# Routed experts in a fused attention and mixture-of-experts kernel: a hold on SP's queue before the second expert's second matrix, one packed load of the counts, and the third block's transposes moved behind the second block

## Chip, core and metric

The kernel runs on one core of one Trainium2 chip. The metric is the time of one execution on the device in microseconds; less is better.

## What is computed

Three stages follow one another: windowed attention over 1152 tokens, a dense mixture of four experts, and a routed mixture of eight experts. The change touches the third stage alone, which in the reference is (cut):

```python
    skip_score = x @ w_skip
    do_compute = skip_score > 0
    out = x.copy()
    ...
    xc = x[do_compute]
    logits = xc @ w_gate
    e_idx = np.argmax(logits, axis=1)
    ...
    for e in range(E):                       # E = 8
        mask = e_idx == e
        ...
        h = np.maximum(xc[mask] @ w1[e], 0.0)    # 512 -> 1024
        y[mask] = gate_w[mask, None] * (h @ w2[e])   # 1024 -> 512
    out[do_compute] = xc + y
```

How many tokens an expert gets is known only on the chip. All matrices are float32.

## The kernel before

**Tiling.** Each float32 operand is split in a high and a low part (`xs` for tokens, `wa1h`/`wa1l`, `wa2h`/`wa2l`, `wb1h`... for weights), and a product is made of three passes of TensorE. Experts use two sets of weight tiles in turn: even experts `wb`, odd ones `wa`. A matrix comes from memory in four loads of 512 KB (lines L314 and L316, tile `raw`, issued by SP); ScalarE casts each load to the high part (L330) and VectorE subtracts to get the low part (L334).

**Blocks.** The routed tokens of an expert are taken in blocks of 128 rows. A block is: gather its rows from the scratch tensor `scr` by an indirect DMA of GpSimd (L869; tile `xg` for an expert's first and second block, `xj` for its third), transpose them on TensorE (L362, four instructions), split them into `xs` (L896 on ScalarE, L898 on VectorE), first product (L920), ReLU into `hr` (L944, ScalarE), transpose `hr` (L961), split into `ht` (L965, L968), second product (L920 again), scale and add (L1004), and scatter to the output (L877, GpSimd). In a block, 24 matmuls of the first product in two halves of 12 come with two groups of transposes of `hr` and 24 matmuls of the second product. An expert's second and third block stand in `tc.If`: `over(e, i)` tests if the expert has more than 64 times i rows. A block with at most 64 rows takes a smaller variant. In this execution experts 1, 2 and 4 have a second block (small for expert 2), and expert 4 alone a third one (small).

**Order.** A planner (`Plan`) collects operations with priorities and estimated durations and writes each engine's instructions in the order of its estimated starts when `plan.run()` is called; each engine then runs its own queue strictly in order and waits for semaphores. One call covers an expert's first block together with the loads and splits of the next expert's weights; each conditional block is planned by itself. The rows of the third block were transposed in the conditional second block by `amid`, which puts them into the plan between that block's two products, with priority 11.5 and a dependence on `("g2", 2)`. As names of the plan are forgotten at each `plan.run()` and the second product is added later, that dependence names nothing there, and the priority (the groups of the first product have 11, 12, ...) decides the place.

**Counts.** VectorE writes three packed numbers to `cnt`: the levels of all experts, whether any expert has over 384 rows, and the same or a second block of the last expert. `counts` (L1072) loads each into a register on all five engines. The branches read them. `ahead` gives TensorE's sequencer a hint on the coming branch.

**Around the change.** When routing is done, at about 488 us, the first block of expert 0 starts at once with rows that were picked on TensorE. In parallel GpSimd issues seven gathers, the first of them for expert 1's first block. SP issues the four loads of expert 1's second matrix (`raw2` buffers, L316), and after the branch of expert 0 the four loads of expert 2's first matrix (L314).

## Time and profile before

| | us |
|---|---|
| median of 3 runs | 666.32 (663.26 to 671.25) |
| the profiled execution: its time | 669.26 |
| the profiled execution: its span | 667.5 |
| PE busy | 632.6 (95%) |
| DVE busy | 314.6 (47%) |
| ACT busy | 234.5 (35%) |
| POOL busy | 75.5 (11%) |

The profile comes from one execution. PE is TensorE's matmuls, PEld its weight loads, DVE VectorE, ACT ScalarE, POOL GpSimd, and SP the engine that only issues DMAs; a "q" behind a name is the engine's sequencer. A wait's releaser is inferred from semaphores; "remote" is a release whose origin the profile doesn't tell. The granted clock is TensorE's, as a share of 2.4 GHz; 0.5 is 1.2 GHz. Idle time counts only where the engine is the one that the end waits for.

### The profile page before, as it was taken

To read this page: it belongs to the slowest core of one execution; us is meant where nothing else is said; L and a number is where in the kernel's file an instruction comes from. 1 tells how busy PE (TensorE), PEld (TensorE's weight loads), DVE (VectorE), ACT (ScalarE), POOL (GpSimd) and SP (SyncE) were. 2 spreads that over 40 slices of the span, in tenths; PEclk is the share of its full clock that TensorE was granted. 3 is DMA by queue.
4 is the path that set the end of the run, shared out by engine and by line. 5 is a ranking of instruction groups with operands and counts; after the bars stand their busy time and mean duration, and the time that the engine had idled before them with its cause. 6 is when DMAs were issued, how large, how long until landed. Compare 5 with 4: busy or idle time off the path is not lost. (4 is left out here: it accounts for less than half of the span.)

```text
span 667.5 us, 9890 instructions
## 1 busy us (share of the span) xinstructions
PE 632.6 (95%) x3787; PEld 553.6 (83%) x3787; DVE 314.6 (47%) x683; ACT 234.5 (35%) x488; POOL 75.5 (11%) x104
## 2 busy tenths in 40 slices
PE   8889999999999999999999999999997899969974
PEld 6688898898989898989898989889876677858864
DVE  5878731127412125412125426165856564931961
ACT  5668630026302024202023311114326464823741
POOL 3112320000000000000000000000123122230510
PEclk9989999999999999999999999999997899979987
DMA  9892100006400004300003310010559864970730
GB/s 217 208 286 66 33 3 1 0 1 229 149 1 1 0 1 130 122 1 0 1 1 126 127 64 33 31 64 13 190 177 373 302 188 159 325 281 18 236 108 11
DMA packets 55770, 71.44 MB, mean 107 GB/s; under 512 B 32932, under 2 KB 32932, under 8 KB 55696
## 3 DMA queue, kind: packets, MB, share of 16 engines
q1 hardware_dynamic: 52912, 62.17, 29.5%
q0 software_dynamic: 2784, 8.30, 4.3%
q8 instruction: 43, 0.70, 0.4%
q14 instruction: 31, 0.25, 0.1%
HBM read 63.74 MB, written 7.47 MB: 107 GB/s over the span
## 5 line engine op out<-in xcount | busy, mean ns | idle before, releaser
L523 PE MATMUL mm<-xth,wa1h 128*128 128x384 f32 (+1 forms) x416 | 137.6, 331 | 0.0
L523 PE MATMUL mm<-xtl,wa1h 128*128 128x384 f32 (+1 forms) x416 | 135.8, 327 | 0.0
L523 PE MATMUL mm<-xth,wa1l 128*128 128x384 f32 (+1 forms) x416 | 135.7, 326 | 0.0
L529 ACT ACTIVATE hh<-mm 128x384 fp32r<-128x384 f32 (+1 forms) x104 | 48.4, 466 | 236.2 <-PE mm L523 231.2
L544 PE MATMUL mm<-wa2h,hh 128*128 128x512 f32 (+1 forms) x296 | 117.3, 396 | 0.0
L531 DVE SCALAR_TENSOR_TENSOR hl<-mm,hh 128x384 fp32r<-128x384 f32 (+1 forms) x104 | 54.6, 526 | 128.4 <-ACT hh L529 128.1
L544 PE MATMUL mm<-wa2h,hl 128*128 128x512 f32 (+1 forms) x296 | 115.1, 389 | 0.0
L544 PE MATMUL mm<-wa2l,hh 128*128 128x512 f32 (+1 forms) x296 | 115.0, 388 | 0.0
L523 PEld LDWEIGHTS mm<-xth,wa1h 128*128 128x128 f32 x416 | 79.0, 190 | 0.6 <-issue 0.2
L523 PEld LDWEIGHTS mm<-xtl,wa1h 128*128 128x128 f32 x416 | 78.9, 190 | 0.4
L523 PEld LDWEIGHTS mm<-xth,wa1l 128*128 128x128 f32 x416 | 78.9, 190 | 0.0
L544 PEld LDWEIGHTS mm<-wa2h,hl 128*128 128x128 f32 x296 | 55.7, 188 | 12.4
L544 PEld LDWEIGHTS mm<-wa2h,hh 128*128 128x128 f32 x296 | 55.8, 188 | 11.2
L544 PEld LDWEIGHTS mm<-wa2l,hh 128*128 128x128 f32 x296 | 55.8, 189 | 11.0
L556 DVE SCALAR_TENSOR_TENSOR x<-mm,prob,x 128x512 f32<-128x512 f32 x24 | 18.0, 751 | 86.8 <-PE mm L544 86.8
L781 POOL DMA_INDIRECT x<-scr,id x1 | 2.0, 1970 | 385.0 <-DVE id L798 385.0
L334 DVE TENSOR_TENSOR wa2l<-raw,wa2h 128x1024 fp32r<-128x1024 f32 x32 | 38.6, 1218 | 7.8 <-ACT wa2h L330 7.8
L330 ACT CAST wa2h<-raw 128x1024 fp32r<-128x1024 f32 x32 | 33.0, 1051 | 25.9 <-PE mm L544 18.6
L334 DVE TENSOR_TENSOR wa1l<-raw,wa1h 128x1024 fp32r<-128x1024 f32 x32 | 38.6, 1236 | 2.1 <-ACT wa1h L330 2.1
L330 ACT CAST wa1h<-raw 128x1024 fp32r<-128x1024 f32 x32 | 32.0, 1048 | 17.4 <-DMA raw<-in_moe_w_dram 9.1
L968 DVE SCALAR_TENSOR_TENSOR ht<-pt,ht 128x512 fp32r<-128x512 f32 (+2 forms) x27 | 15.1, 568 | 36.4 <-ACT ht L965 32.7
L920 PE MATMUL mm<-wa1h,xs 128*128 128x512 f32 (+1 forms) x60 | 22.4, 437 | 6.9 <-issue 3.5
(209 smaller groups left out, 887.4 us busy)
## 6 DMA issues: line engine op xcount, KB each, us to landing
raw<-in_moe_w_dram SPq DMA_DIRECT2D x96, 512.0 KB, 5.9
qn<-in_q_dram SPq DMA_DIRECT2D x8, 256.0 KB
kn<-in_k_dram SPq DMA_DIRECT2D x8, 256.0 KB, 5.9
vn<-in_v_dram SPq DMA_DIRECT2D x8, 256.0 KB
scr<-x SPq DMA_DIRECT2D x8, 256.0 KB
out_dram<-x SPq DMA_DIRECT2D x8, 256.0 KB, 2.3
qn<-in_q_dram SPq DMA_DIRECT2D x2, 128.0 KB, 3.3
kn<-in_k_dram SPq DMA_DIRECT2D x2, 128.0 KB
```

What stands on the lines that cost most here:

```text
L330: (POOL.tensor_copy if hpool else DVE.tensor_copy if hdve else ACT.copy)(out=aps()[0], in_=b.tile)
L334: (POOL if pool else DVE).tensor_tensor(out=l, in0=b.tile, in1=f32(h), op=ALU.subtract)
L523: PE.matmul(out=ps[:, 0:n], lhsT=wa[a][:, kk, f * 128:(f + 1) * 128], rhs=x[:, kk, g0:g0 + n], start=(i == 0), stop=(i == 3 * KC - 1))
L529: add("ACT", c_act(n), lambda: ACT.activation(out=hh[:, f, 0:n], in_=ps[:, 0:n], func=ACTF.Relu), rd=[ps], wr=[("hh", f)], prio=-1)
L531: add("DVE", c_dve(n), lambda: DVE.scalar_tensor_tensor(out=hl[:, f, 0:n], in0=ps[:, 0:n], scalar=0.0, in1=f32(hh[:, f, 0:n]), op0=ALU.max ...
L544: PE.matmul(out=ps[:, 0:c1 - c0], lhsT=x[:, f, o:o + 128], rhs=wa[a][:, f, c0:c1], start=(f == 0 and i == 0), stop=(f == FC - 1 and i == 2))
L556: DVE.scalar_tensor_tensor(out=z, in0=y, scalar=prob[:, t, e:e + 1], in1=z, op0=ALU.mult, op1=ALU.add)
L781: add("POOL", 1.0, lambda: POOL.indirect_dma_start(out=R["x0"], out_offset=None, in_=scr[0:128 * (GT + 1), :], in_offset=bass.IndirectOffs ...
L920: PE.matmul(out=ps[:, 0:cols.stop - cols.start], lhsT=op(k), rhs=ring[f"{c}{a}"][:, k, cols], start=(n == 0 and k == ks[0] and a == "h"), ...
L968: add("DVE", c_dve(w * n), lambda: DVE.scalar_tensor_tensor(out=ht[:, s, n:2 * n], in0=p[:, 0:w, 0:n], scalar=0.0, in1=f32(ht[:, s, 0:n]), ...
```

## The change

Four edits in the routed stage. A one-element DMA (`hold`) from the gathered rows of expert 1's first block into a scratch tensor `pins` is put on SP's queue ahead of expert 1's second matrix, and the gather of those rows is named earlier in the code (it stays the first on GpSimd's queue). The three register loads become one, and the two flags are worked out from the packed levels by register arithmetic (`many`, `further`); `num` on VectorE loses two instructions, and the load's planned place is earlier (`slack` 1.5 for 4.0). The third block's transposes are added behind the second block, in the full variant as before, and depend on the fourth group of the second product, `("g2", 3)`. The gathers' loop skips the one that was named earlier.

```diff
+    pins = scr_p.tile([128, 16], F32, name="pins")
...
-            DVE.tensor_reduce(out=sm[:, 1:2], in_=x[:, 5], axis=AX.X, op=ALU.max)
-            DVE.tensor_tensor(out=sm[:, 2:3], in0=sm[:, 1:2], in1=x[:, 1, E2 - 1:E2], op=ALU.max)
...
-            DVE.tensor_copy(R["cnt"][0:1, E2:E2 + 3], sm)
+            DVE.tensor_copy(R["cnt"][0:1, E2:E2 + 1], sm)
...
         w_pass("r", 1, 1)
+        xgs[1, 0] = gather(1, 0)
+
+        def hold():
+
+            SP.dma_start(out=pins[0:1, 0:1], in_=xgs[1, 0].tile[0:1, 0:1])
+
+        add("SP", 0.5, hold, rd=[xgs[1, 0]], wr=["MR"], slack=-2.5)
         w_pass("r", 1, 2)
...
         def counts():
-            for i, m in ((E2, 8 ** E2 - 1), (E2 + 1, 1), (E2 + 2, 1)):
-                nv.append(nc.values_load(R["cnt"][0:1, i:i + 1], min_val=0, max_val=m,
-                                         skip_runtime_bounds_check_because="levels of all experts, packed"))
+            nv.append(nc.values_load(R["cnt"][0:1, E2:E2 + 1], min_val=0, max_val=8 ** E2 - 1,
+                                     skip_runtime_bounds_check_because="levels of all experts, packed"))
+
+        def many():
+
+            return (nv[0] >> 1) & (nv[0] >> 2) & sum(8 ** e for e in range(E2))
...
-            def gathered():
-                if e == E2 - 1:
-                    xgs[e, 2] = gather(e, 2)
-                third["xt"] = xpose(xgs[e, 2], 11.5, [("g2", 2)])
-
             with tc.If(over(e, 2 * j + 1)) as c:
-                block(e, j, x, xt, amid=gathered if j == 1 else None)
+                if j == 1 and e == E2 - 1:
+                    xgs[e, 2] = gather(e, 2)
+                block(e, j, x, xt)
+                if j == 1:
+                    third["xt"] = xpose(xgs[e, 2], 11.5, [("g2", 3)])
...
-            return nv[2] > 0 if e == E2 - 1 else over(e, 2)
+            return (many() | (nv[0] & (6 * 8 ** e))) > 0 if e == E2 - 1 else over(e, 2)
...
-                    with tc.If(nv[1] > 0):
+                    with tc.If(many() > 0):
                         deep()
...
-                add("X", 0.0, counts, rd=["cnt"], wr=["nv"], slack=4.0)
+                add("X", 0.0, counts, rd=["cnt"], wr=["nv"], slack=1.5)
...
-                    if e + d < E2:
+                    if e + d < E2 and (e + d, j) not in xgs:
```

TensorE's queue in the second block of expert 1 (`xs` its rows, `xj` the third block's), before, from the third matmul of the first product to the transposes of `hr`:

```order
L920 MATMUL mmx<-wa1h,xs 128x512
L920 MATMUL mmx<-wa1l,xs 128x512
L362 MATMUL pt<-ident,xj 128x128 [waits DMASW5_49,PE_49]
L362 MATMUL pt<-ident,xj 128x128 x3
L920 MATMUL mmx<-wa1h,xs 128x512
L920 MATMUL mmx<-wa1l,xs 128x512
L920 MATMUL mmx<-wa1h,xs 128x512
L920 MATMUL mmx<-wa1l,xs 128x512
L920 MATMUL mmx<-wa1h,xs 128x512 x5
L920 MATMUL mmx<-wa1l,xs 128x512
L920 MATMUL mmx<-wa1h,xs 128x512
L920 MATMUL mmx<-wa1l,xs 128x512
L961 MATMUL pt<-ident,hr 128x128 [waits DVE_49,Activation_49]
```

And in the changed kernel, at the end of the same block's second product, up to the branch on a third block:

```order
L920 MATMUL mmx<-wa2h,ht 128x512 [waits Activation_49]
L920 MATMUL mmx<-wa2l,ht 128x512
L920 MATMUL mmx<-wa2h,ht 128x512
L920 MATMUL mmx<-wa2l,ht 128x512
L364 MATMUL pt<-ident,xj 128x128 [waits DMASW5_49,PE_49]
L364 MATMUL pt<-ident,xj 128x128 x3
L920 MATMUL mmx<-wa2h,ht 128x512
L920 MATMUL mmx<-wa2l,ht 128x512
L920 MATMUL mmx<-wa2h,ht 128x512
L920 MATMUL mmx<-wa2l,ht 128x512
L920 MATMUL mmx<-wa2h,ht 128x512 [waits DVE_49]
L920 MATMUL mmx<-wa2h,ht 128x512 x3
```

The transposes with their wait for the gather (`DMASW5`) stood behind the fourth matmul of the block; they now stand behind the fortieth of 48, with eight matmuls to follow.

SP's queue behind the last rows of the dense stage, before (`raw` with a number are the four loads of expert 1's second matrix):

```order
L316 DMA raw_4271<-in_moe_w_dram 128x2x512 [waits DMAHW1_49,DMAHW0_49,DMAHW3_49,DMASW0_49,DMAHW4_49,PE_49,DMAHW7_49,Activation_49,Pool_49]
L316 DMA raw_4291<-in_moe_w_dram 128x2x512
L1072 TENSOR_LOAD cnt [waits DMAHW2_49,DMAHW3_49,DMAHW1_49,DMAHW4_49,DMAHW0_49,DMAHW5_49,DVE_49,DMAHW6_49,PE_49,DMAHW7_49,Activation_49,Pool_49]
L1072 TENSOR_LOAD cnt x2
L316 DMA raw_4331<-in_moe_w_dram 128x2x512
L316 DMA raw_4363<-in_moe_w_dram 128x2x512 [waits DMAHW2_49]
```

And in the changed kernel, at the same place:

```order
L1078 TENSOR_LOAD cnt [waits DMAHW2_49,DMAHW3_49,DMAHW1_49,DMAHW4_49,DMAHW0_49,DMAHW5_49,DVE_49,DMAHW6_49,PE_49,DMAHW7_49,Activation_49,Pool_49]
L1070 DMA pins<-xg 1x1 [waits DMAHW3_49,DMAHW1_49,DMAHW4_49,DMAHW0_49,DMAHW7_49,DMASW1_49,PE_49]
L318 DMA raw_4363<-in_moe_w_dram 128x2x512 [waits PE_49,DMASW0_49,Activation_49,Pool_49]
L318 DMA raw_4378<-in_moe_w_dram 128x2x512
L318 DMA raw_4382<-in_moe_w_dram 128x2x512 [waits DMAHW2_49]
L318 DMA raw_4387<-in_moe_w_dram 128x2x512
```

All four loads, and whatever SP issues after them, now stand behind a wait for the first gather (`DMASW1`).

## Rows read from the trace of the kernel before

**Rows 1.** Stretches; busy us (x) of PE, PEld, DVE, ACT, POOL; granted clock; DMA share; GB/s

```profile
0.00:488.00 488.00, 479.13 (x3035) 427.73 (x3035) 212.45 (x529) 149.07 (x366) 28.81 (x69) 1.00 0.25 73
488.00:668.00 180.00, 153.48 (x754) 125.88 (x752) 102.15 (x154) 85.41 (x123) 46.71 (x35) 0.92 0.59 199
```

**Rows 2.** Waits of PE: who for whom; us in total, times, longest

```profile
PE pt L362 <- DMA xj<-scr,idg: 7.6, 2, 5.1
```

**Rows 3.** Timeline of PE, second block of expert 1; start, duration, [idle before <-releaser]

```profile
520.56 0.40 PE L920 MATMUL mmx<-wa1h,xs 128*128 128x512 f32 x1
...
524.13 1.09 PE L362 MATMUL pt<-ident,xj 128*128 128x128 f32 x4 [2.48 <-DMA xj<-scr,idg]
...
528.96 0.65 PE L961 MATMUL pt<-ident,hr 128*128 128x128 f32 x4
```

**Rows 4.** Timeline of PE, second block of expert 4

```profile
588.43 0.39 PE L920 MATMUL mmx<-wb1h,xs 128*128 128x512 f32 x1
...
594.65 1.09 PE L362 MATMUL pt<-ident,xj 128*128 128x128 f32 x4 [5.13 <-DMA xj<-scr,idg]
...
600.01 0.60 PE L961 MATMUL pt<-ident,hr 128*128 128x128 f32 x4
```

**Rows 5.** Timeline of PE, first block of expert 3, and the transposes in it

```profile
562.19 0.39 PE L920 MATMUL mm<-wa1h,xs 128*128 128x512 f32 x1
...
565.89 0.64 PE L961 MATMUL pt<-ident,hr 128*128 128x128 f32 x4
...
569.16 0.60 PE L362 MATMUL pt<-ident,xg 128*128 128x128 f32 x4
569.59 0.60 PE L961 MATMUL pt<-ident,hr 128*128 128x128 f32 x4
```

**Rows 6.** Stretches after two of the waits, columns as in rows 1

```profile
505.00:510.00 5.00, 5.00 (x12) 3.95 (x13) 4.96 (x8) 3.61 (x4) 1.02 (x1) 0.50 1.03 361
...
595.00:600.00 5.00, 5.00 (x16) 3.99 (x15) 0.69 (x1) 1.22 (x2) 0.00 (x0) 0.58 0.21 82
```

**Rows 7.** Timeline of PE, first block of expert 1

```profile
500.90 0.60 PE L362 MATMUL pt<-ident,xg 128*128 128x128 f32 x4
504.89 0.80 PE L920 MATMUL mm<-wa1h,xs 128*128 128x512 f32 x1 [3.39 <-ACT xs L896]
...
511.34 0.63 PE L961 MATMUL pt<-ident,hr 128*128 128x128 f32 x4
```

**Rows 8.** Timeline of ACT, the same stretch

```profile
504.23 0.61 ACT L896 CAST xs<-pt 128x512 fp32r<-128x512 f32 x1 [7.26 <-remote]
504.73 3.88 ACT L330 CAST wa2h<-raw 128x1024 fp32r<-128x1024 f32 x4
510.48 0.60 ACT L944 ACTIVATE hr<-mm 128x512 f32<-128x512 f32 x1 [1.87 <-PE mm L920]
```

**Rows 9.** Timeline of SP: loads of expert 1's second matrix, expert 2's first

```profile
492.49 3.38 SPq L316 DMA_DIRECT2D raw<-in_moe_w_dram  x4
496.49 1.82 SPq L314 DMA_DIRECT2D raw<-in_moe_w_dram  x4
```

**Rows 10.** Timeline of POOL: first gather of the routed part, and the one for rows 3

```profile
493.96 0.96 POOL L869 DMA_INDIRECT xg<-scr,idg  x1 [12.19 <-DVE g L742]
...
515.63 0.94 POOL L869 DMA_INDIRECT xj<-scr,idg  x1 [0.30 <-issue]
```

**Rows 11.** DMA queues from 500 to 508 us: packets, MB, share of 16 engines

```profile
q1 hardware_dynamic: 506, 1.59, 54.7%
q0 software_dynamic: 393, 1.29, 47.2%
```

**Rows 12.** Timeline of DVE: low parts of expert 2's second matrix

```profile
521.43 4.62 DVE L334 TENSOR_TENSOR wb2l<-raw,wb2h 128x1024 fp32r<-128x1024 f32 x4
```

**Rows 13.** Line L1072, the loads of counts into registers; ns min/median/max, first and last start

```profile
L1072 PEldq TENSOR_LOAD <-cnt x3: 305/307/498, 494.1 to 495.2; - x3
```

**Rows 14.** Line L1129, branches of PE's sequencer, columns as in rows 13

```profile
L1129 PEldq COMPARE_BRANCH  x8: 76/360/3028, 499.2 to 656.3; - x8
```

More of the change, by code (lines that the diff above doesn't have):

```diff
@@ L231, in fused_kernel @@
     scr = scr_p.tile([NT, DM], F32, name="scr")
+    pins = scr_p.tile([128, 16], F32, name="pins")
+    npin = [0]
     xlast = const.tile([128, DM], F32, name="xj", tag="xj", bufs=1)
@@ L583, in open_routing @@
                            ("wr", [128, KC, E2 + 1], F32), ("os0", [128, E2], BF16), ("os1", [128, E2], BF16),
-                           ("cnt", [128, E2 + 3], I32), ("idg", [128, TT, E2], U32), ("ids", [128, TT, E2], U32), ("id0", [128, 1], U32), ("x0", [128, DM], F32),
+                           ("cnt", [128, E2 + 1], I32), ("idg", [128, TT, E2], U32), ("ids", [128, TT, E2], U32), ("id0", [128, 1], U32), ("x0", [128, DM], F32),
                            ("gates", [128, TT, E2], F32), ("tb", [128, TT, 2, E2], F32),
                            ("a", [128, TT, E2], F32), ("b", [128, TT, E2], F32), ("lvw", [1, E2], F32),
-                           ("lvt", [1, 6, E2], F32), ("lvx", [1, 6, E2], F32), ("lvs", [1, 3], F32)):
+                           ("lvt", [1, 6, E2], F32), ("lvx", [1, 6, E2], F32), ("lvs", [1, 1], F32)):
             R[nm] = (rt_p if nm in ("tri", "ones", "iota_s", "iota_e", "jlow", "tok1", "wr", "id0", "x0") else rc_p).tile(
@@ L818, in num @@
             DVE.tensor_tensor(out=x, in0=n.unsqueeze(1).to_broadcast([1, 6, E2]), in1=R["lvt"], op=ALU.is_gt)
-            DVE.tensor_reduce(out=sm[:, 1:2], in_=x[:, 5], axis=AX.X, op=ALU.max)
-            DVE.tensor_tensor(out=sm[:, 2:3], in0=sm[:, 1:2], in1=x[:, 1, E2 - 1:E2], op=ALU.max)
             DVE.scalar_tensor_tensor(out=x, in0=x, scalar=1.0, in1=R["lvw"].unsqueeze(1).to_broadcast([1, 6, E2]),
                                      op0=ALU.mult, op1=ALU.mult, accum_out=sm[:, 0:1])
-            DVE.tensor_copy(R["cnt"][0:1, E2:E2 + 3], sm)
+            DVE.tensor_copy(R["cnt"][0:1, E2:E2 + 1], sm)
             DVE.tensor_copy(R["cnt"][0:1, 0:E2], n)
-        add("DVE", 1.0, num, rd=["pf"], wr=["cnt"], prio=16)
+        add("DVE", 0.7, num, rd=["pf"], wr=["cnt"], prio=16)
     def route_gates():
@@ L1082, in rows @@
             third = {}
-            def gathered():
-                if e == E2 - 1:
+            with tc.If(over(e, 2 * j + 1)) as c:
+                if j == 1 and e == E2 - 1:
                     xgs[e, 2] = gather(e, 2)
-                third["xt"] = xpose(xgs[e, 2], 11.5, [("g2", 2)])
-            with tc.If(over(e, 2 * j + 1)) as c:
-                block(e, j, x, xt, amid=gathered if j == 1 else None)
+                block(e, j, x, xt)
+                if j == 1:
+                    third["xt"] = xpose(xgs[e, 2], 11.5, [("g2", 3)])
                 if j == 0:
```

## Prediction

> **What bounds the kernel now.** I read the stretches first. In the dense part, up to 488 us, PE is busy 479.1 of 488.0 us at a granted clock of 1.00; in the routed part it is busy 153.5 of 180 us at 0.92 [rows 1]. No edit reaches the dense part. So the gain has to come from 26.5 us in which PE stands still and from what runs at less than the full clock in the routed part. Next I read whom PE waits for. The largest entry that the change addresses is the third block's transposes waiting for their gather: 7.6 us in two waits, the longest 5.1 [rows 2]. Then I read PE's own order of work at those two places [rows 3, 4] and at a block of the same form without such a wait [rows 5], for the price of a wait is more than the wait: behind it the clock is lower. Between 595 and 600 us the granted clock is 0.58, and between 505 and 510 us, behind another wait, 0.50, which is 1.2 GHz of 2.4 [rows 6]. Last come SP, GpSimd, ACT and VectorE around 493 to 526 us, where the hold works [rows 7 to 12].
>
> **The transposes.** A block's form is fixed: 16 matmuls stand between its first one and the first transposes of `hr`. Without a wait this takes 565.89 − 562.19 = 3.70 us, 0.23 a matmul [rows 5]. In expert 1's second block it takes 528.96 − 520.56 = 8.40 us [rows 3], in expert 4's 600.01 − 588.43 = 11.58 [rows 4]. Between stand four additional transposes, which move but do not vanish; at full clock four take 569.59 − 569.16 = 0.43 us [rows 5]. So the wait with its slow stretch costs 8.40 − 3.70 − 0.43 = 4.27 us in the first place (2.48 is the wait, 1.79 the clock) and 11.58 − 3.70 − 0.43 = 7.45 in the second (5.13 and 2.32). Only these two blocks count: of the experts with a second block only 1 and 4 have a full one, which alone carries the transposes.
>
> At the new place 40 matmuls and two groups of transposes stand ahead, some 40 × 0.23 + 2 × 0.43 = 10.1 us from the block's start. The gathers landed at 524.13 and 594.65, where PE's waits ended [rows 3, 4], which is 3.6 and 6.2 us into those blocks. They are there by then with 4 us to spare, so both waits go: **−4.27 and −7.45 us**.
>
> What is late next? Behind the moved transposes eight matmuls remain, 8 × 0.23 = 1.85 us, for the split of the third block's rows; ACT's half of such a split takes 0.61 us [rows 8], VectorE's follows it. Two such steps are 1.2, which with the passing on between engines just fits. It counts for expert 4 alone, the one with a third block. Between 0 and 0.3, I take **+0.1**. In expert 1's second block something nearer comes up. VectorE is at the low parts of expert 2's second matrix from 521.43 to 526.05 [rows 12], and that stands in its queue ahead of this block's `ht`. A block without a wait would have its transposes of `hr` at 520.56 + 3.70 = 524.26, be through the last eight matmuls of the first product at 524.26 + 0.43 + 1.85 = 526.5, and want `ht` then; VectorE's part of `ht`, about as long as the 0.6 us of ACT, could start at 526.05 and end at 526.7. That is **+0.2**, and one us more for each by which those splits slip.
>
> **The hold.** Before, SP issues the second matrix of expert 1 from 492.49 and the first of expert 2 from 496.49 [rows 9]; the first gather is issued at 493.96 [rows 10]. Where the rows arrive is seen from one side: the transposes that read them run at 500.90 with no wait of their own [rows 7]. So they land between 494.9 and 500.9; I take 498, and SP's four loads, 2.1 MB, start then instead of at 492.5. When is the last one there? At 361 GB/s, the rate of all queues from 505 to 510 us [rows 6], after 5.8 us, at 503.8; at what q1 got beside the gathers and scatters from 500 to 508 us, 1.59 MB in 8 us [rows 11], after 10.5, at 508.5. The latter is the queue and the stretch in question, so I take 508.5.
>
> Who waits for them? ACT's queue has `xs` at 504.23, then the four casts of that matrix (3.88 us, 0.97 each), and only then `hr`, at 510.48; `tr(hr)`, as I call the transposes of `hr`, follows 0.86 us later, at 511.34 [rows 7, 8]. A last load at 508.5 gives `tr(hr)` at 508.5 + 0.97 + 0.86 = 510.3. What would PE alone need? Its transposes end at 501.5, but its next matmul waits 3.39 us for `xs`, up to 504.89 [rows 7], and then runs at 1.2 GHz; without that wait `tr(hr)` would stand at 501.5 + 0.7 + 3.70 = 505.9. So if the hold removes this wait, the loads put another in its place, from 505.9 to 510.3, with a slow clock behind it as behind the other two (1.79 and 2.32, say 2.0): 510.3 − 511.34 + 2.0 = +1.0. If it does not remove it, PE is the later one and the hold costs 0. The ends are −5.4 (no stall at all: 505.9 − 511.34) and +2.0 (last load at 509.5). I take **+0.5**, since the trace does not show why `xs` started so late: its row names a releaser of unknown origin, not a DMA [rows 8].
>
> **Counts.** A load of a count into a register takes PE's sequencer 305 to 498 ns [rows 13]; two fewer are 0.6 us. But they ran from 494.1 to 495.7 while PE's array worked through its queue, and no wait of PE is put down to them. I take 0 (at best −0.6); the two fewer instructions of VectorE lie in the same cover. The new flags need some six more register instructions at the last expert. With the cheapest branch of that sequencer, 76 ns [rows 14], as the upper bound for one: 0 to 0.46, **+0.25**.
>
> The Trainium skill (DMA: Bandwidth & Descriptors, section "Latency and other measured facts") gives such a load a floor of about 600 ns. The rows show half of that. By the page the edit takes 1.2 us off each engine instead of 0.6; the sum would be the same, as neither stands on the path.
>
> **Sum.** −4.27 − 7.45 + 0.1 + 0.2 + 0.5 + 0.25 = −10.7 us. Against the profiled execution's own 669.26 that is 658.6. This execution is 2.9 us longer than the median of the runs, 666.32; part of its waits may be missing in the others, or not. From the median the sum gives 655.6; I go between: **657 us**.
>
> **Rivals.** Times are like the forecast's, 657, with the term changed.
>
> *The hold pays.* If the loads land by 504, or if the stall at 501.5 came from them, −5.4 takes the place of +0.5: 651. For it: DMA engines at a share of 1.03 from 505 to 510 [rows 6], so transfers press each other here. Against: the casts stand in order ahead of `hr`, and a load that is sent later is not there sooner. Chance 0.16.
>
> *The hold delays expert 2's splits.* Eight loads, 4.2 MB, now follow from 498; at q1's 0.20 MB/us the last would land near 519, and the splits that VectorE now ends at 526.05 would end 3 to 4 us later, ahead of `ht` in expert 1's second block. The −4.27 there is then given back, nearly all: 661. For it: VectorE has only 0.5 us to spare there. Against: a queue whose neighbours are done moves more than 0.20. Chance 0.15.
>
> *PE's sequencer stalls at a branch.* Its branches at L1129 take 76 to 3028 ns, the median 360 [rows 14]. The change shifts all code behind the counts and adds instructions, so another branch may take 3 us. With 2.0 for the clock behind it that is 662. Against: the change may as well remove the one that is there. Chance 0.09.
>
> The Trainium skill speaks for such stalls (Runtime: NRT & Kernel Launch, section "Instruction fetch mechanics"): a taken branch whose target is not in the window of code that is present has to wait for a DMA of it.
>
> *Slower.* One mechanism can do it: SP behind the hold. Each us by which expert 1's second matrix lands after 509.5 delays `tr(hr)` by one us. The kernel is back at its old time when the other terms (−11.2) and the clock (+2.0) are used up, with the last load at 518.7, and over 1% slower from 525.4. The longest gather in these rows took from 515.63 [rows 10] to 524.13 [rows 3], 8.5 us; from 493.96 that is 502.5, and the loads would land at 513. Even so the kernel gains 6 us. It needs both a gather and loads twice as slow: 675, chance 0.04.
>
> **Chances and range.** The forecast has 0.56. A difference of 1%, 6.7 us, is about what a measurement of this kernel tells from no change: faster means below 659.7. The forecast (0.56, of which 0.04 may reach past 659.7) and the paying hold (0.16) lie there, 0.68 in all; late splits (0.15), the branch (0.09) and the forecast's rest lie within 1%, 0.28; 0.04 is slower. The range takes 650.5 to 662.5: the paying hold, late splits and the branch fit in, with half a us at either side; the slower case and the far parts of the others stay out.
>
> **What would show it.** In the changed kernel PE has no wait of `pt` for `xj`, and both second blocks reach `tr(hr)` about 3.7 us after their first matmul, with a granted clock near 1.00. SP's loads of expert 1's second matrix start near 498, and ACT's casts of `wa2` wait for `raw`, or they do not and the hold was early. PE's wait for `xs` near 501.5 is gone or still there. VectorE's `ht` in expert 1's second block waits behind `wb2l` by under 0.5 us. The prediction is wrong if the transposes wait at their new place, if the waits' cost turns up again behind them, or if expert 1's first block ends more than 2 us from where it ended.

## The result, and the profile after

The changed kernel takes 660.29 us (median of 20 runs, 658.43 to 665.42), the kernel before 666.76 (20 runs, 662.97 to 672.10). The ratio is 0.9905, with a 95% interval of 0.9885 to 0.9925: 6.5 us less, just under the 1% that the prediction called faster (below 659.7), to which it had given 0.68. 660.29 lies in its range of 650.5 to 662.5, and 3.3 us above its 657.

Two of PE's waits in the changed kernel (who for whom; us in total, times, longest), beside [rows 2]:

```profile
PE pt L961 <- DVEq L1138: 5.3, 1, 5.3
...
PE mm L920 <- ACT xs L896: 1.4, 1, 1.4
```

No wait for `xj` is left. A wait of 5.3 us for VectorE's sequencer, at the transposes of `hr` (L961), is new; the wait for `xs` has gone from 3.4 to 1.4. The stretches (busy us and number of instructions of PE, PEld, DVE, ACT, POOL; granted clock; DMA share; GB/s), cut where expert 0's first matmul starts, and one behind the new wait:

```profile
0.00:485.60 485.60, 478.09 (x3035) 426.35 (x3035) 212.88 (x529) 149.53 (x366) 28.89 (x69) 1.00 0.26 73
485.60:657.00 171.40, 148.83 (x752) 122.78 (x752) 102.48 (x152) 85.81 (x122) 47.71 (x35) 0.95 0.62 209
510.00:515.00 5.00, 4.54 (x15) 3.81 (x16) 2.99 (x4) 2.88 (x4) 3.60 (x3) 0.58 1.03 393
```

In [rows 1] the routed part begins at 488 us, here at 485.6; the dense part happened to be shorter, which no edit touches. Positions are therefore counted from expert 0's first matmul from here on (488.14 in the first profile of before, 486.80 in the second, 485.62 here). PE in the changed kernel, expert 1's first block and its second (start, duration, [idle before <-releaser]), as in [rows 7] and [rows 3]:

```profile
501.22 0.51 PE L920 MATMUL mm<-wa1h,xs 128*128 128x512 f32 x1 [1.41 <-ACT xs L896]
...
510.46 1.09 PE L961 MATMUL pt<-ident,hr 128*128 128x128 f32 x4 [5.26 <-DVEq L1138]
...
521.39 0.40 PE L920 MATMUL mmx<-wa1h,xs 128*128 128x512 f32 x1
...
525.10 0.64 PE L961 MATMUL pt<-ident,hr 128*128 128x128 f32 x4
```

And expert 4's second block, as in [rows 4]:

```profile
584.64 0.39 PE L920 MATMUL mmx<-wb1h,xs 128*128 128x512 f32 x1
...
588.34 0.64 PE L961 MATMUL pt<-ident,hr 128*128 128x128 f32 x4
...
594.82 0.60 PE L364 MATMUL pt<-ident,xj 128*128 128x128 f32 x4
```

Both second blocks now reach the transposes of `hr` 3.71 and 3.70 us behind their first matmul; before it was 8.40 and 11.58. The transposes of `xj` stand at the end and wait for nothing. But in expert 1's first block the transposes of `hr` stand 24.84 us behind expert 0's first matmul, where [rows 7] gives 511.34 − 488.14 = 23.20. SP, ACT and VectorE show what precedes them, as in [rows 8, 9]:

```profile
495.09 0.29 SPq L1070 DMA_DIRECT2D pins<-xg  x1
495.55 2.29 SPq L318 DMA_DIRECT2D raw<-in_moe_w_dram  x4
```

```profile
501.41 1.05 ACT L332 CAST wa2h<-raw 128x1024 fp32r<-128x1024 f32 x1 [0.25 <-DMA raw<-in_moe_w_dram]
504.14 1.05 ACT L332 CAST wa2h<-raw 128x1024 fp32r<-128x1024 f32 x1 [1.68 <-DMA raw<-in_moe_w_dram]
506.61 1.04 ACT L332 CAST wa2h<-raw 128x1024 fp32r<-128x1024 f32 x1 [1.42 <-DMA raw<-in_moe_w_dram]
507.96 1.05 ACT L332 CAST wa2h<-raw 128x1024 fp32r<-128x1024 f32 x1 [0.30 <-DMA raw<-in_moe_w_dram]
509.18 0.60 ACT L944 ACTIVATE hr<-mm 128x512 f32<-128x512 f32 x1 [0.18 <-ACTq L1138]
```

```profile
507.69 2.57 DVE L336 TENSOR_TENSOR wa2l<-raw,wa2h 128x1024 fp32r<-128x1024 f32 x2 [1.24 <-ACT wa2h L332]
```

The hold lets SP go at 495.09, the loads land one by one until 507.9, and each cast on ACT waits for its load. VectorE ends the last low part at 507.69 + 2.57 = 510.26, and PE starts at 510.46. ACT's `hr` itself was done at 509.78. The same distance stands in the first profile of before, where VectorE's low parts ended at 506.52 + 4.62 = 511.14 and PE's transposes of `hr` began at 511.34 [rows 7]:

```profile
506.52 4.62 DVE L334 TENSOR_TENSOR wa2l<-raw,wa2h 128x1024 fp32r<-128x1024 f32 x4
```

The table sums up all kernels. Columns: ratio to before; then the time from expert 0's first matmul to the transposes of `hr` in expert 1's first block, the start of its second block, the start of expert 2 and the start of expert 4's third block, each read from PE's timeline of one execution.

| kernel | ratio (95%) | hr 1 | second block | expert 2 | third block |
|---|---|---|---|---|---|
| before, first profile | 1 | 23.20 | 32.42 | 49.97 | 120.11 |
| before, again | | 20.85 | 30.07 | 49.61 | 117.21 |
| changed | 0.9905 (0.9885 to 0.9925) | 24.84 | 35.77 | 49.08 | 111.50 |
| move_alone | 0.9824 (0.9794 to 0.9854) | 20.98 | 31.76 | 47.11 | 108.17 |
| hold_alone | 1.0003 (0.9979 to 1.0027) | 25.94 | 36.50 | 49.83 | 119.66 |
| counts_alone | 0.9978 (0.9955 to 1.0000) | 20.05 | 29.27 | 49.80 | 120.08 |
| no_hold | 0.9818 (0.9793 to 0.9843) | 20.51 | 30.02 | 45.44 | 107.94 |
| late_count | 0.9800 (0.9769 to 0.9831) | 19.48 | 28.70 | 44.11 | 106.50 |
| hold_later | 0.9916 (0.9889 to 0.9943) | 26.91 | 38.69 | 51.98 | 113.82 |
| hold_dve | 0.9926 (0.9899 to 0.9953) | 25.77 | 36.96 | 50.25 | 112.77 |
| hold_split | 0.9895 (0.9860 to 0.9930) | 20.65 | 31.43 | 46.98 | 109.55 |
| nohold_split | 0.9802 (0.9768 to 0.9837) | 17.87 | 27.09 | 43.62 | 106.27 |
| hold_filled | 0.9991 (0.9967 to 1.0014) | 25.91 | 35.13 | 48.44 | 119.64 |
| hold_next | 0.9838 (0.9805 to 0.9870) | 20.34 | 29.56 | 44.90 | 107.49 |

### The profile page after: what moved, and what is told of

Same layout as the page of the kernel before. It is cut to its first block, busy times and chain, and to the rows that moved or that the text cites. A ratio compares the mean times of both kernels' runs of the same rounds, so it can differ in the third digit from the quotient of the medians.

```text
span 657.1 us, 9915 instructions
## 1 busy us (share of the span) xinstructions
PE 626.9 (95%) x3787; PEld 549.1 (84%) x3787; DVE 315.4 (48%) x681; ACT 235.3 (36%) x488; POOL 76.6 (12%) x104
## 5 line engine op out<-in xcount | busy, mean ns | idle before, releaser
L546 PEld LDWEIGHTS mm<-wa2h,hl 128*128 128x128 f32 x296 | 55.7, 188 | 12.4
```

The source lines that it names most:

```text
L546: PE.matmul(out=ps[:, 0:c1 - c0], lhsT=x[:, f, o:o + 128], rhs=wa[a][:, f, c0:c1], start=(f == 0 and i == 0), stop=(f == FC - 1 and i == 2))
```

## The experiments: the change taken apart

**The changed kernel without the hold.**

```diff
-        add("SP", 0.5, hold, rd=[xgs[1, 0]], wr=["MR"], slack=-2.5)
```

> The changed kernel without the hold; the moved transposes and the single count load stay. Theory A, the hold costs time: relative to the start of expert 0's first block, expert 1's second block began 3.35 us later in the changed kernel than before, so without the hold the kernel should be about 3 us faster than with it: a ratio to before of 0.984 to 0.987 (the changed kernel has 0.9905), with PE's wait for the transposes of hr in expert 1's first block gone or under 2 us. Theory B, the hold pays: PE waits for xs fell from 3.39 to 1.41 us with it, so without it the ratio is 0.992 to 0.996 and a wait for xs of about 3.4 us is back.

Measured: 0.9818, 654.88 us (5 runs). The hold costs 0.9905 / 0.9818 = 1.0089, 5.9 us (about 2 us to either side by the two intervals), which is more than theory A's 3 us. The two traces place it: expert 1's second block starts 5.75 us later with the hold (35.77 for 30.02), expert 2 only 3.64 (49.08 for 45.44). Without the hold 1.46 us go into a wait for `hr` in that second block, and 0.5 us more into PE's branch in front of expert 2. At the end the two executions are 5.5 us apart, since 1.5 us come in the last expert: in the 4 us behind a wait of 3.62 us the granted clock is 0.58 in the changed kernel, behind one of 3.23 us it is 1.00 without the hold. PE's wait at the first transposes of `hr` is 2.21 us, and the one in the second block stands below it:

```profile
509.23 0.63 PE L961 MATMUL pt<-ident,hr 128*128 128x128 f32 x4 [2.21 <-DVEq L1137]
...
524.07 0.66 PE L961 MATMUL pt<-ident,hr 128*128 128x128 f32 x4 [1.46 <-ACT hr L944]
```

Theory B falls: without the hold there is no wait of 3.4 us for `xs`.

**The moved transposes alone**, on the kernel before.

```diff
-            def gathered():
...
-                block(e, j, x, xt, amid=gathered if j == 1 else None)
+                if j == 1 and e == E2 - 1:
+                    xgs[e, 2] = gather(e, 2)
+                block(e, j, x, xt)
+                if j == 1:
+                    third["xt"] = xpose(xgs[e, 2], 11.5, [("g2", 3)])
```

> Only the third block's transposes moved; SP's queue and the counts as before. Theory A: the waits of both second blocks go and nothing else happens, -4.7 and -7.9 us as in the changed kernel's trace, less up to 1 us given back in front of ht: a ratio of 0.982 to 0.986. Theory B: in most executions the gathers land earlier than in the one that was profiled, and the move alone is worth what the whole change is: 0.989 to 0.992.

Measured: 0.9824, −11.7 us (−9.7 to −13.7), as theory A says. This edit alone is worth nearly twice what the whole change is worth. In its trace 2.0 us of the gain are given back already: PE's branch in front of expert 2 takes 2.42 us, where it takes 0.37 in the kernel before, and from expert 1's second block to expert 2 pass 15.35 us, in the changed kernel 13.31.

**The hold alone**, with the gather that it waits for, on the kernel before.

```diff
...
+        xgs[1, 0] = gather(1, 0)
...
+            SP.dma_start(out=pins[0:1, 0:1], in_=xgs[1, 0].tile[0:1, 0:1])
+
+        add("SP", 0.5, hold, rd=[xgs[1, 0]], wr=["MR"], slack=-2.5)
...
-                    if e + d < E2:
+                    if e + d < E2 and (e + d, j) not in xgs:
```

> Only the hold, with the gather named earlier; transposes and counts as before. Theory A: 3 us slower, a ratio of 1.003 to 1.006, and PE waits 4 to 6 us in front of the first transposes of hr in expert 1's first block. Theory B: 0.995 to 0.999. A third outcome, that delay in expert 1's first block is taken off the wait for xj in its second, would give 1.000 to 1.002, with the wait for xj under 1 us there.

Measured: 1.0003. The third outcome came: a wait of 7.9 us is there, and the kernel is no slower. PE in expert 1's first block, and at the transposes of `xj` in its second:

```profile
512.08 1.09 PE L962 MATMUL pt<-ident,hr 128*128 128x128 f32 x4 [7.93 <-DVEq L1137]
...
523.57 0.60 PE L363 MATMUL pt<-ident,xj 128*128 128x128 f32 x4
```

The wait for `xj` is gone from expert 1's second block, because PE reached it later (that block starts at 36.50, for 32.42 and 30.07 before) and the gather had landed. Expert 2 starts at 49.83, as it does in the kernel before (49.97 and 49.61) and with the counts alone (49.80). So as long as the transposes of `xj` stood early, the gather decided when expert 2 began, and what was lost ahead of it was covered; here the delay has just used the cover up. The move of the transposes takes this cover away, and then the hold has a price.

**The counts alone**, on the kernel before.

```diff
...
-            for i, m in ((E2, 8 ** E2 - 1), (E2 + 1, 1), (E2 + 2, 1)):
...
+            nv.append(nc.values_load(R["cnt"][0:1, E2:E2 + 1], min_val=0, max_val=8 ** E2 - 1,
...
-                add("X", 0.0, counts, rd=["cnt"], wr=["nv"], slack=4.0)
+                add("X", 0.0, counts, rd=["cnt"], wr=["nv"], slack=1.5)
```

> Only the packed load of the counts with its earlier place. In the changed kernel's trace PE stands still for 0.72 us at that load, behind the first transposes of hr of expert 0, and 1.31 us lie there between instructions that are otherwise 0.36 apart. Theory A: the early place costs 0.9 us on PE, a ratio of 1.000 to 1.002, with that gap in the trace. Theory B: it costs nothing or gains, 0.998 to 1.000.

Measured: 0.9978 (0.9955 to 1.0000), by time at the lower edge of theory B, and with the gap of A in the trace. The count load of PE's sequencer, in the changed kernel (ns min/median/max, first and last start), and the matmul behind it, there and in this run:

```profile
L1078 PEldq TENSOR_LOAD <-cnt x1: 487/487/487, 490.2 to 490.2; - x1
```

```profile
491.04 0.50 PE L920 MATMUL mm<-wb1h,xs 128*128 128x512 f32 x1 [0.72 <-issue]
```

```profile
493.22 0.50 PE L920 MATMUL mm<-wb1h,xs 128*128 128x512 f32 x1 [0.72 <-issue]
```

The load is about as long as the longest in [rows 13], and is not hidden: in the changed kernel 1.31 us pass from the transposes at 489.73 to the next matmul, where 0.36 pass in the kernel before. Against it a branch of PE's sequencer became short (below). Neither is seen in the end of this execution: expert 2 starts at 49.80, as in the kernel before, and the routed part takes 180.0 us, for 179.4 and 178.1 in the two profiles of before. Why the median is 1.5 us less is not shown.

**The kernel before, once more.**

> The kernel before, unchanged, profiled a second time. The prediction took the 3.39 us wait for xs at the start of expert 1's first block as part of it. If that wait is an accident of one execution, it is under 1.5 us here and the first transposes of hr in that block stand 20 to 21.5 us behind expert 0's first matmul (23.2 in the first profile); if it belongs to the kernel, it is over 3 us and they stand at 23 again. The wait for xj in expert 1's second block then absorbs the difference: expert 2 starts 49.5 to 50.5 us behind expert 0 in both cases.

```profile
501.12 0.49 PE L920 MATMUL mm<-wa1h,xs 128*128 128x512 f32 x1 [1.00 <-PEq L1129]
...
507.65 0.63 PE L961 MATMUL pt<-ident,hr 128*128 128x128 f32 x4 [2.56 <-DVEq L1129]
...
522.48 0.63 PE L362 MATMUL pt<-ident,xj 128*128 128x128 f32 x4 [4.52 <-DMA xj<-scr,idg]
```

The transposes of `hr` stand at 20.85, in the predicted band. The wait of 3.39 us in [rows 7] was thus an accident of that execution. VectorE stood still there too, until 504.08, with the same unnamed releaser as ACT; why both began so late stays open. The wait for `xj` is 4.52 us here instead of 2.48: the gather lands when it lands, and expert 2 starts at 49.61.

**The hold on the third gather.**

```diff
+        xgs[1, 1] = gather(1, 1, 0.5)
+        xgs[2, 0] = gather(2, 0, 0.6)
...
-            SP.dma_start(out=pins[0:1, 0:1], in_=xgs[1, 0].tile[0:1, 0:1])
+            SP.dma_start(out=pins[0:1, 0:1], in_=xgs[2, 0].tile[0:1, 0:1])
...
-        add("SP", 0.5, hold, rd=[xgs[1, 0]], wr=["MR"], slack=-2.5)
+        add("SP", 0.5, hold, rd=[xgs[2, 0]], wr=["MR"], slack=-2.5)
```

> The changed kernel with SP's hold on the third gather instead of the first, which GpSimd issues about 2.8 us later. Theory (the hold delays the last load of expert 1's second matrix and everything behind its casts on ACT, us for us): PE's wait in front of the first transposes of hr grows from 5.26 to 6.5 to 8 us and the ratio to before goes from 0.9905 to 0.992 to 0.9955. Rival (the loads are slow because gathers run beside them, so that a later start is made up): the wait stays at 4.5 to 5.5 us and the ratio at 0.989 to 0.992.

Measured: 0.9916 (0.9889 to 0.9943), which doesn't separate the two. The trace does: SP issues the hold at 499.56, which is 11.45 us behind expert 0's first matmul, against 9.47 in the changed kernel, 1.98 later; the transposes of `hr` come 2.07 later, and the third block 2.3. In these two traces the price goes with the start of the loads, nearly us for us. The wait, 8.62 us, is longer than expected, since PE had no wait for `xs` in that execution:

```profile
515.02 1.09 PE L961 MATMUL pt<-ident,hr 128*128 128x128 f32 x4 [8.62 <-DVEq L1140]
```

## The experiments: through which engine the hold costs

**Two casts on VectorE.**

```diff
-            w_split(b, ring, key, p, c, prio + st * c, pool=(kd, e, p) == ("m", 0, 2) and KN["w2pool"][c],
+            w_split(b, ring, key, p, c, prio + st * c, hdve=(kd, e, p) == ("r", 1, 2) and c > 1, pool=(kd, e, p) == ("m", 0, 2) and KN["w2pool"][c],
```

> The changed kernel, hold and all, with the casts of the third and fourth load of expert 1's second matrix on VectorE instead of ACT, so that only two casts stand ahead of hr on ACT. Theory (the price of the hold comes through ACT's order): the wait of 5.26 us in front of the first transposes of hr falls to under 1.5 us, and of the hold's price of 5.9 us 2 to 4.5 come back, since VectorE's longer queue now holds ht: a ratio of 0.9835 to 0.9875. Rival (PE needs the held matrix itself as soon as ACT does): the time is the same within 1.5 us, 0.988 to 0.993, and the wait moves to the second product.

Measured: 0.9926 (0.9899 to 0.9953), in the rival's band by time; both expectations are wrong on the wait, which got longer. ACT, VectorE and PE:

```profile
505.51 0.60 ACT L944 ACTIVATE hr<-mm 128x512 f32<-128x512 f32 x1 [0.18 <-ACTq L1138]
```

```profile
509.69 2.35 DVE L336 TENSOR_TENSOR wa2l<-raw,wa2h 128x1024 fp32r<-128x1024 f32 x2
```

```profile
512.25 1.09 PE L961 MATMUL pt<-ident,hr 128*128 128x128 f32 x4 [7.46 <-DVEq L1138]
```

ACT has `hr` ready at 506.1, but PE's transposes of it start at 512.25, 0.2 us after VectorE's last low part (509.69 + 2.35 = 512.04). The releaser is VectorE's branch (L1138). Between the first block of expert 1 and that of expert 0 lies the branch on expert 0's second block; VectorE reaches it only when the splits ahead of it are done, and what PE waits for is a semaphore's count that VectorE's sequencer adds behind the branch. So the prediction's chain "casts ahead of `hr` on ACT" was not the one that decides; the low parts and the branch on VectorE are: in the changed kernel PE starts at 510.46, and ACT's chain would have let it start at 509.18 + 0.86 = 510.04. (The casts that were moved make VectorE's own queue longer here, so this run shows which engine is last, not what the hold costs through it.)

**Two splits behind the branch, with the hold.** (The third and fourth split of expert 1's second matrix are planned with expert 1's block; a slack of 2.0 goes to the splits of expert 2's first matrix.)

```diff
-    npass = [0]
+    npass, w2late = [0], []
...
+            if (kd, e, p) == ("r", 1, 2) and c >= 2 and len(w2late) < 2:
+                w2late.append(lambda b=b, c=c: w_split(b, ring, key, p, c, 9.0 + 0.1 * c, slack=3.5))
+                continue
...
-                    after=["idg"] if kd == "r" and e == 1 and p == 2 else [], slack=7.0 if kd == "r" and e == 1 and p == 2 else 0.0)
+                    after=["idg"] if kd == "r" and e == 1 and p == 2 else [], slack=7.0 if kd == "r" and e == 1 and p == 2 else 2.0 if (kd, e, p) == ("r", 2, 1) else 0.0)
...
+            if e == 1:
+                for f in w2late:
+                    f()
             block(e, 0, xgs[e, 0], xts[e, 0])
```

> The changed kernel with its hold, but the splits (cast on ACT, low part on VectorE) of the third and fourth load of expert 1's second matrix are planned with expert 1's block, behind the branch, and expert 2's first casts up to 2 us later in the plan. In the run with two casts moved to VectorE, ACT's hr ran at 505.51, but PE's transposes of it only at 512.25, let go by VectorE's branch, in front of which all four low parts stand. Revised theory: the hold's price comes through the branch, which VectorE and ACT reach only behind the splits. Then PE's wait in front of the first transposes of hr falls from 5.26 to under 2 us, and of the hold's 5.9 us at least 3 come back: a ratio of 0.981 to 0.986. Rival: PE needs the late loads themselves, in the second product: the wait moves there, 0.988 to 0.992.

Measured: 0.9895 (0.9860 to 0.9930), no better than the changed kernel and in the rival's band by time. At the disputed place the trace speaks for the branch theory: the wait falls from 5.26 to 2.38 (under 2 was expected), and the second block starts 4.3 us earlier (31.43 for 35.77). Half of it is lost again in the second block:

```profile
506.37 0.63 PE L961 MATMUL pt<-ident,hr 128*128 128x128 f32 x4 [2.38 <-DVEq L1141]
...
523.10 0.66 PE L961 MATMUL pt<-ident,hr 128*128 128x128 f32 x4 [2.08 <-ACT hr L944]
```

```profile
518.12 1.05 ACT L332 CAST wb2h<-raw 128x1024 fp32r<-128x1024 f32 x1 [0.91 <-DMA raw<-in_moe_w_dram]
520.16 1.05 ACT L332 CAST wb2h<-raw 128x1024 fp32r<-128x1024 f32 x1 [0.98 <-DMA raw<-in_moe_w_dram]
521.51 1.04 ACT L332 CAST wb2h<-raw 128x1024 fp32r<-128x1024 f32 x1 [0.30 <-DMA raw<-in_moe_w_dram]
522.46 0.59 ACT L944 ACTIVATE hr<-mmx 128x512 f32<-128x512 f32 x1
```

ACT's casts of expert 2's second matrix wait for their loads, in order ahead of `hr` of expert 1's second block. This is near the prediction's second rival: SP's later loads are late too, once nothing earlier hides it. But it is not the hold's doing alone, since the same wait is there without a hold (1.46 us in `no_hold`, 0.80 in `nohold_split`). In the trace 2.1 us of the hold's price come back (expert 2 at 46.98 for 49.08).

**The same without the hold**, the count load at its old place.

```diff
-        add("SP", 0.5, hold, rd=[xgs[1, 0]], wr=["MR"], slack=-2.5)
...
-                add("X", 0.0, counts, rd=["cnt"], wr=["nv"], slack=1.5)
+                add("X", 0.0, counts, rd=["cnt"], wr=["nv"], slack=4.0)
```

> The same two splits behind the branch, without the hold and with the count load at its old place (the kernel that had 0.980). If the branch theory holds, the 1.46 us that PE still waits there go too: 0.976 to 0.979. If expert 2's weights or PE's own branch are next to be late, it stays at 0.979 to 0.982.

Measured: 0.9802 (0.9768 to 0.9837), in the second band. PE no longer waits at the first transposes of `hr` (17.87 for 19.48 in `late_count`), and the time doesn't change. Expert 2 starts 0.5 us earlier instead of 1.6: in expert 1's second block 0.80 us go to a wait for `hr`, and PE's branch in front of expert 2 takes 2.64 us (2.48 in `late_count`).

**The hold one step later**, ahead of expert 2's first matrix.

```diff
-        add("SP", 0.5, hold, rd=[xgs[1, 0]], wr=["MR"], slack=-2.5)
...
+            if e == 1:
+                add("SP", 0.5, hold, rd=[xgs[1, 0]], prio=-9)
             block(e, 0, xgs[e, 0], xts[e, 0])
```

> The changed kernel with SP's hold one step later: behind expert 1's second matrix, ahead of expert 2's first. Theory: a load that is waited for later has room for a hold: expert 1's first block is as without any hold, and expert 2's first matrix, some 2 to 3 us later, costs at most 1 us: 0.981 to 0.984. If the loads compete, expert 1's second matrix lands earlier and it gains: 0.977 to 0.981. Rival (ACT's casts for expert 2 stand in order ahead of ht and hr, so that any hold on a load costs): 0.985 to 0.990.

Measured: 0.9838 (0.9805 to 0.9870), as the theory says: a hold in front of loads that are waited for later costs at most little (without it 0.9818). Expert 1's first block is as without a hold (20.34 for 20.51). ACT waits there for the last load of expert 1's second matrix until 17.83 us, without a hold until 18.00, though SP issues expert 2's loads 4.5 us later (10.95 for 6.48). This speaks against expert 2's loads as what makes expert 1's slow.

**Work in the wait.** Twenty matmuls are added; the first four of the second half of expert 1's first product are done six times, each time anew.

```diff
-                    for k in ks:
+                    again = 5 if (e, j, name, n) == (1, 0, "g14", 0) else 0
+                    for k, left in [(k, left) for left in range(again, -1, -1) for k in ks]:
...
-                                      stop=(n == len(groups) - 1 and k == ks[-1] and a == ws[-1]))
+                                      stop=((n == len(groups) - 1 or left > 0) and k == ks[-1] and a == ws[-1]))
```

> The changed kernel with 20 more matmuls on PE ahead of the first transposes of hr in expert 1's first block: the first four of the second half are done six times, each time started anew, so that the last time stands. They take 4.6 us at full clock, inside the wait of 5.26. Theory (a wait costs its length and then a slow stretch): the transposes come no later, the clock behind them stays at 1.00, and from them to expert 1's second block pass 9.5 us instead of 10.9: 0.987 to 0.990. Rival (the slow stretch is not the wait's doing): 0.990 to 0.993, with matmuls 0.43 apart behind the transposes as before.

Measured: 0.9991, far from both, though the mechanism shows. The stretch behind the wait, columns as above:

```profile
512.00:517.00 5.00, 5.00 (x28) 4.34 (x29) 3.36 (x4) 4.26 (x8) 1.89 (x2) 1.00 1.04 387
```

The clock is 1.00 where it was 0.58 (the last of the stretches of the changed kernel), and from the transposes to the second block pass 9.22 us for 10.93. So the slow stretch behind the wait was worth 1.71 us, and it goes when a part of the wait is filled. A wait of 3.00 us is left even so:

```profile
511.98 0.63 PE L962 MATMUL pt<-ident,hr 128*128 128x128 f32 x4 [3.00 <-DVEq L1139]
```

(Here the loads were later by chance, the wait ended 1.07 us later, and still the second block started 0.64 us earlier.) The length of a wait alone does not tell if a slow stretch follows: at the same place the clock stayed at 1.00 behind a wait of 2.56 us in `before_again`, and was 0.66 in the 5 us behind a wait of 2.56 us in `move_alone`. The time was lost elsewhere. From expert 1's second block to expert 4's third pass 84.5 us, in the changed kernel 75.7. Two branches of PE's sequencer, on expert 2's second block and in front of expert 4, more than account for these 8.8 us (ns min/median/max; lines are those of that kernel's code):

```profile
L1095 PEldq COMPARE_BRANCH  x7: 68/239/5775, 518.3 to 641.7; - x7
```

```profile
L1139 PEldq COMPARE_BRANCH  x8: 73/344/6158, 496.8 to 650.2; - x8
```

The longest take 5.8 and 6.2 us. In the changed kernel no branch in that part takes over 0.4 us. Ahead of the last expert it is the other way round: two branches that take 3.10 and 3.14 us in the changed kernel take 0.44 and 0.24 here, which gives back 4 us. All that was added is 20 matmuls, some 35 and 60 us ahead of the two long branches.

**The packed count load at its old place, without the hold.**

```diff
-                add("X", 0.0, counts, rd=["cnt"], wr=["nv"], slack=1.5)
+                add("X", 0.0, counts, rd=["cnt"], wr=["nv"], slack=4.0)
```

> The changed kernel without the hold and with the packed count load at the planned place of before (slack 4.0 for 1.5). If PE's gap of 0.72 us at the early load is all it costs, the kernel gains 0.9 us against the one without the hold: a ratio to before of 0.979 to 0.982 (0.9818 without the hold), and PE has no issue wait behind the first transposes of hr of expert 0. If the early load has a use (gathers or branches earlier), it is 0.982 to 0.985.

Measured: 0.9800 (0.9769 to 0.9831), 654.65 us, in the first band. The gap behind the transposes of `hr` of expert 0 is gone (0.36 us). The interval overlaps that of `no_hold`, so the gain of 1 us between them is read from the trace (expert 2 at 44.11 for 45.44) and not shown by time. These two, and `move_alone`, `nohold_split` and `hold_next`, are faster than both kernels of this case.

## Why the prediction came out as it did

**What bounds the kernel, and the wait for `xj`: right.** The waits named were the ones that went.

**The transposes, −4.27, −7.45, +0.1 and +0.2, together −11.4: right.** The move alone measured −11.7 (−9.7 to −13.7); that the two are so close is in part luck, as 2.0 us went into a branch in that execution. In the traces the way from expert 1's second block to expert 2 fell from 49.97 − 32.42 = 17.55 to 49.08 − 35.77 = 13.31 us in the changed kernel, −4.24, and expert 4's second block, from its start to that of the third, from 19.82 to 12.48, −7.34. The second profile of before divides the sum in another way (6.23 and 4.80) and gives nearly the same, 11.0, which is why the sum held although each wait varies from run to run. Working out a wait as the wait and the slow clock behind it was right as well: 1.71 us was measured in `hold_filled`, where 1.79, 2.32 and "say 2.0" had been taken; that a slow stretch follows every such wait was not.

**The hold, +0.5: this step failed.** It costs 5.9 us (about 2 to either side). By the prediction's own sign, a first block of expert 1 that ends over 2 us from where it ended, the step is wrong: counted from expert 0's first matmul it ends 3.35 us later than in the first profile of before (35.77 for 32.42), and 5.70 later than in the second. The mechanism was named in the main (loads late, splits in order, PE's transposes of `hr` waiting), with the wrong engine at its end; four terms of it were off, three of them to the same side:

- The place to compare with. `tr(hr)` at 511.34 contained the accidental wait of 3.39 for `xs`. The second profile has it at 20.85 us behind expert 0, not 23.20: 2.35 us.
- The last load. It was put at 508.5, 10.5 us behind the start at 498. In the changed kernel SP starts them 9.93 us behind expert 0's first matmul (495.55 − 485.62), where the estimate had 9.9, but they take 12.4 us to 507.9: 1.9 us more. The rate of q1 in one stretch was too good for these four loads; `hold_next` speaks against the loads of expert 2 as the cause, so what made them slow stays open.
- The engine. PE waits for VectorE's branch behind the low parts, not for ACT's `hr`: 510.46 − 507.96 = 2.50 us from the start of the last cast, where 0.97 + 0.86 = 1.83 was taken: 0.7 us. The prediction read 511.34 as 0.86 us behind ACT's `hr`; VectorE's low parts ended 0.20 us before it in the same trace.
- The slow stretch was 1.7, not 2.0: −0.3 us.

Taken from 20.85, the changed kernel's 24.84 and 1.71 give 5.7 us, which is the delay at the start of expert 1's second block (5.75 against `no_hold`). That it equals the 5.9 by time is in part luck, since only 3.64 of it reach expert 2. The prediction said itself that the trace did not show why `xs` started late, and yet took that wait into its base; it chose a value near nothing because one of the two cases it weighed was "the wait stays", and a wait that is not there in other runs can't stay.

A second thing was hidden in that base: in the kernel before the hold costs nothing that can be measured (`hold_alone`, 1.0003), since the wait for `xj` behind it swallows the delay. The edits were added up as if they were independent, but one of them takes away the cover of the other.

**The counts, 0 and +0.25: small, as forecast, and not for the reason given.** The rows of the load were read at its old place, where PE had work in its queue; the diff moves it to a place where it costs PE 0.95 us. In return the branch on expert 0's second block got short (next section). Measured together they give 0.9978 (0.9955 to 1.0000), −1.5 us with no change at the edge of the interval; no step in the trace of that run shows where the 1.5 us would come from.

**The sum.** −10.7 against the profiled execution's 669.26 gave 658.6, and the changed kernel's profiled execution took 658.81; the two agree only because that execution of before held 2.35 us of accident and the changed one had a dense part 2.5 us shorter and is among the shortest of its runs. Counted from expert 0's first matmul the changed execution is 7.9 us shorter than the first profile of before and 6.6 shorter than the second. Between the medians lie 6.5 us, 4.2 less than the sum's 10.7: the hold's term was 5.4 too small (5.9 for 0.5), the counts gave 1.75 more than their term (−1.5 for +0.25) and the move 0.3, which leaves 3.4; the rest is within the intervals. The step to 657 covered a part of that, since it stood 1.4 above what the sum gives from the median. So the time lies in the range with one term wrong by 5.4 us: a range that also held the late splits and the branch was wide enough for it.

**The rivals.** "The hold pays" is refuted. "The hold delays expert 2's splits" is true of the queue, but hidden behind the earlier wait; a wait of this kind shows in `hold_split`, and a shorter one without the hold. "PE's sequencer stalls at a branch": no new stall came in the changed kernel (the two of 3.1 us ahead of the last expert are 3.0 and 2.9 in the kernel before), and two came in `hold_filled`, where they cost more than the whole change brings. "Slower" needed the last load at 518.7; it came at 507.9.

## What to carry to other kernels

When two edits act on one path, ask whether the wait that one removes is the cover of the other's delay: alone the hold cost nothing, beside the moved transposes 5.9 us, and the change without it is worth 12 us instead of 6.5. Before a wait of the profile goes into the base of a sum, see whether a second execution has it too, above all if its releaser can't be named. When PE is released by another engine's branch, look at the work of that engine in front of the branch. Moving some of it behind the branch cut PE's wait here (5.26 to 2.38 us), though not the time, which the next wait took.

## What the runs showed of the hardware

**PE's branches.** A branch of PE's sequencer takes 0.3 us in the changed kernel (median of 18), but some take 1.7 to 3.9 us: the same ones in the two profiles of the kernel before, and not the same ones in every kernel. The one on expert 0's second block took 2.80 and 3.07 us in the two profiles of before, 2.98 in `move_alone`, 2.69 in `late_count`, 2.57 in `nohold_split`, and under 0.5 in the changed kernel and all others. The one behind expert 1's second block took 0.37 before, 0.38 in the changed kernel, 0.86 in `no_hold`, which came to it at 44.5 us, and 2.4 to 2.6 in `move_alone`, `hold_next`, `late_count` and `nohold_split`, which came to it at 44.6, 42.4, 41.6 and 40.9. In `late_count`:

```profile
L1104 PEldq COMPARE_BRANCH  x3: 75/351/2484, 523.9 to 589.2; - x3
```

That gives back a part of what is gained ahead of it, though the time at which PE arrives does not explain it alone, as 44.5 and 44.6 show. The profile lists code as DMA traffic of its own (queue, packets, MB, share of 16 engines; from the changed kernel's page):

```profile
q8 instruction: 43, 0.70, 0.5%
```

The Trainium skill (Runtime: NRT & Kernel Launch, section "Instruction fetch mechanics") says that a taken branch to code that isn't at hand waits for a DMA of it. Stalls of 1.7 to 6.2 us that change with the code agree with it; which code is at hand, and whether these stalls are such waits, no run here shows.

**A semaphore's count that passes a branch.** PE waited in `hold_dve` for 6.1 us with its operand ready (ACT's `hr` ended at 506.1, PE began at 512.25), because the count it waits for is completed by VectorE's sequencer at the branch, behind the low parts that wait for the held loads.

**A count load is short, and in the way.** 0.26 to 0.56 us of a sequencer each in both kernels, hidden on PE in the kernel before, where PE's matmuls run on beside it, and paid for with 0.95 us of PE at its earlier place in the changed kernel.
